# x handed over in both layouts, and LayerNorm's factor applied behind the V, Q and K products

## The chip, the cores and the metric

One NeuronCore of a Trainium2 chip runs the whole program. Its engines are TensorE (PE, with PEld for its weight loads), VectorE (DVE), ScalarE (ACT), GpSimd (POOL) and SyncE (SP), whose queue issues all DMAs here. The metric is the device time of one execution in microseconds (us), lower is better.

## The reference

A transformer block on x of 2048 tokens by 640 features, in float32: pre-LayerNorm sliding-window attention, then a gated MLP. The change touches only the first LayerNorm and the three products behind it.

```python
def _layernorm(x, axis=-1, eps=1e-5):
    m = jnp.mean(x, axis=axis, keepdims=True)
    v = jnp.var(x, axis=axis, keepdims=True)
    return (x - m) / jnp.sqrt(v + eps)

# _A_ref, given x = _layernorm(x): H = 32 heads of Dh = 20, window W = 256
qkv = (x @ wqkv).reshape(B, S, 3, H, Dh).transpose(2, 0, 3, 1, 4)
q, k, v = qkv[0], qkv[1], qkv[2]
scores = einsum("bhqd,bhkd->bhqk", q, k) * Dh ** -0.5   # masked to 0 <= q - k < W
o = einsum("bhqk,bhkd->bhqd", softmax(scores), v)
A = o.transpose(0, 2, 1, 3).reshape(B, S, D) @ wo

h = x + A                                               # A = _A_ref(_layernorm(x))
h2 = h + _B_ref(_layernorm(h))                          # gated MLP, not touched
```

## The kernel before

The order of PE, DVE, ACT and SP is the order of the code (`manual_schedule`); POOL's is set by the framework's scheduler. Each engine works strictly through its list, so an instruction that waits holds all behind it on its engine. That goes for SP too: a DMA that waits for a buffer or for another DMA holds every later one.

Float32 products are made of three matmuls: each operand is split into a high part `hi` (rounded by a copy on ACT) and the rest `lo` (a subtraction on DVE or POOL), and hi*hi, hi*lo and lo*hi are summed in PSUM.

**V stage (0 to 92 us).** The 2048 tokens are 16 tiles of 128. For a tile `load_x` fetches it tokens first; `ln1` takes mean and variance (two `bn_stats`, `bn_aggr`, an addition on DVE, the power -0.5 on POOL) and writes x minus mean times the factor to `xn`; `turn1` transposes `xn` feature first by five PE transposes into two PSUM banks, from which ACT writes `hi` and DVE `lo` (`xn_hi`, `xn_lo`, kept for all tokens); `vgemm` multiplies the tile with Wv, 30 matmuls, and ACT evacuates the two halves. At the start the 640 rows of Wv are split too (`split_wv`, ten pieces). The two halves of the first tile's product wait for these.

**Q and K products (92 to 243 us).** 40 `qk_item`s, for ten blocks `m` of 128 output features and four blocks `c` of 512 tokens: 15 matmuls into one of two PSUM buffers (`pv`). Behind each, `split_qk` splits the result into three bfloat16 parts: ACT (L539), DVE (L541), ACT (L543), POOL (L544), and a store (L547) to the memory tensor `qk_d`. The scores are later taken from `load_stack`'s loads (L299) of `qk_d`. The first 24 items go by block `m`, the last 16 (`dense_tail`) by `c`; among the last, `max_item` makes the first unit's unmasked scores and DVE their row maxima (L339), over a ring of three PSUM banks. Then the main loop of attention starts.

`const`, `tmp` and the like are pools; a `tag` with `bufs=n` is a ring of n buffers, and whoever takes a buffer waits for the last reader of its former content. `tmp` holds the rings `ta` (x tiles, later `sg`), `tb` (`xn`, later `rest`) and `wraw`, `wqh`, `wql` (weights raw, hi, lo).

Of the kernel before, what the change touches and what calls it, by code (L numbers as in the profile page):

```python
# [7 lines left out]
F32 = mybir.dt.float32  # L8
# [25 lines left out]
@with_exitstack  # L34
def block_kernel(ctx, tc, x, wqk, wv, wo, w_in, wsp, bsp, w_out, out):
    nc = tc.nc
# [13 lines left out]
    wo_d = dram.tile([KD, 2, P, D], F32, name="wo_d")  # L50
    r_d = dram.tile([H, S], F32, name="r_d")
    h_d = dram.tile([NT, P, D], F32, name="h_d")
    z1_d = dram.tile([NT, P, FH], F32, name="z1_d")
# [174 lines left out]
    with ExitStack() as ab:  # L228
# [220 lines left out]
        if True:  # L449
# [7 lines left out]

            def ln1(i, between=None):
                xn = tmp.tile([P, D], F32, tag="tb", bufs=2, name=f"xn{i}")
                layernorm(xn, xts.pop(i), D, f"a{i}", between)  # L460
                xns[i] = xn

            def turn1(i):
                xn = xns.pop(i)
                c, o = divmod(i, 4)
                for k0, k1 in ((0, 4), (4, KD)):
                    ps = s2_tile()
                    for k in range(k0, k1):
                        nc.tensor.transpose(ps[:, (k - k0) * P:(k - k0 + 1) * P], xn[:, k * P:(k + 1) * P], ident)
# [3 lines left out]
                    nc.scalar.activation(hi, p3, AF.Copy)  # L473
                    nc.vector.tensor_tensor(out=lo, in0=p3, in1=hi.bitcast(F32), op=OP.subtract)

            def vgemm(i):
                c, o = divmod(i, 4)
                t0 = o * P
                for j in range(2):
                    ps = s1_tile() if j else pv_tile(f"v{i}_{j}")  # L480
                    n0 = j * HD
                    for k in range(KD):
# [5 lines left out]
                    nc.scalar.activation(v4[:, i, 16 * j:16 * j + 16, :DH],  # L488
                                         ps[:, :HD].rearrange("p (h c) -> p h c", c=DH), AF.Copy)

            wqs, raws, after = {}, {}, [iter(())]

            def load_wqk(m):
                raws[m] = tmp.tile([P, KD, P], F32, tag="wraw", bufs=5, name=f"wqraw{m}")
                nc.sync.dma_start(raws[m], wqk[m])
# [9 lines left out]
            def load_wo(k):  # L505
                raws[k] = tmp.tile([P, D], F32, tag="wraw", bufs=5, name=f"woraw{k}")
                nc.sync.dma_start(raws[k], wo[k * P:(k + 1) * P, :])
# [9 lines left out]
            def store_wo(k):  # L517
                for a, t in enumerate(wqs.pop(k)):
                    nc.sync.dma_start(wo_d[k, a], t.bitcast(F32))

            def qk_item(m, c):
                ps = pv_tile(f"qk{m}_{c}")
                hi, lo = wqs[m]
# [12 lines left out]
            def split_qk(m, c, ps):  # L536
                sg = tmp.tile([P, 3, 512], BF16, tag="ta", bufs=3, name=f"sg{m}_{c}")
                rest = tmp.tile([P, 512], F32, tag="tb", bufs=2, name=f"rest{m}_{c}")
                nc.scalar.activation(sg[:, 0, :], ps, AF.Copy)  # L539
                yield  # L540
                nc.vector.tensor_tensor(out=rest, in0=ps, in1=sg[:, 0, :], op=OP.subtract)  # L541
                yield
                nc.scalar.activation(sg[:, 1, :], rest, AF.Copy)  # L543
                nc.gpsimd.tensor_tensor(out=sg[:, 2, :], in0=rest, in1=sg[:, 1, :], op=OP.subtract)  # L544
                T = S // 4
                base = qk_d[m // 5, 0, c // 2, m % 5 * 8, 0, c % 2 * 256:c % 2 * 256 + 256]
                nc.sync.dma_start(bass.AP(tensor=base.tensor, offset=base.offset,  # L547
                                          ap=[[T, P], [2 * 2 * DH * H // 2 * T, 3], [1, 256]]), sg.bitcast(F32))

            halves = [slice(0, HD), slice(HD, D)]  # L550
            load_x(0)
            wv_raw = [tmp.tile([P, D], F32, tag="wraw", bufs=5, name=f"wvraw{k}") for k in range(KD)]
            for j, c in enumerate(halves):
# [12 lines left out]
            for n in range(14):  # L566
                nc.tensor.matmul(warm[:, :P], ident, ident, start=True, stop=True)
            ln1(0)
            split_wv(0, c, nc.vector)
# [5 lines left out]
            for k in (0, 1, 3):  # L575
                split_wv(k, d, nc.gpsimd if k % 2 else nc.vector)
            ln1(1, lambda: [split_wv(k, d, nc.vector) for k in (2, 4)])
            for i in range(NT):
                if i + 3 < NT:
                    load_x(i + 3)  # L580
                if i == 0:
                    vgemm(0)
                    ln1(2, lambda: turn1(1))
                elif i + 2 < NT:
                    ln1(i + 2)
                if i == 1:
# [7 lines left out]
                if 4 <= i <= KD + 3:  # L594
                    store_wo(i - 4)
                if i >= NT - 6 and i < NT - 2:
# [727 lines left out]
```

## Time and profile before

| | us |
|---|---|
| three runs | 1136.86, 1134.21, 1131.7 |
| median | 1134.21 |
| the profiled execution | 1132.73 |
| its span in the profile | 1130.9 |
| PE, DVE, ACT, POOL busy | 1093.7, 732.2, 565.9, 296.6 |

The profile is one execution; its span begins with the first instruction and ends with the last, and 1.8 us of the execution's time lie around it. "Busy" leaves out waiting, register and DMA-issuing instructions. A row of the list in order of time gives start, length, engine, line, operation and tiles, and in brackets the idle time of the engine just before it with what ended it; "x5" are five instructions merged in one row. SPq rows are DMA issues, not transfers. Tile names stand without their numbers.

### The profile page before, as it was taken

What the parts mean: (1) busy time and instruction counts of PE and PEld (TensorE: products, weight loads), DVE (VectorE), ACT (ScalarE), POOL (GpSimd) and SP (SyncE); (2) the same over time, 40 slices, a digit from 0 to 9 for tenths busy, and PEclk for the clock granted to TensorE, in tenths of its full rate; (3) what the DMA queues carried; (4) which work ended last, traced back from release to release, by engine and by line L of the source; (5) the groups of instructions that cost most, each with busy time, mean ns of one, the idle gap of its engine ahead of it and who ended that gap; (6) DMA issues with size and microseconds to landing.
All of it is one profiled execution on the core that took longest, in us unless ns stands there. A gap on an engine that the chain in (4) does not pass through costs nothing.

```text
span 1130.9 us, 28689 instructions
## 1 busy us (share of the span) xinstructions
PE 1093.7 (97%) x11180; PEld 986.3 (87%) x11180; DVE 732.2 (65%) x2060; ACT 565.9 (50%) x1169; POOL 296.6 (26%) x429
## 2 busy tenths in 40 slices
PE   8999999999999999889899999999999899999998
PEld 7998887667887777689799999999999799999998
DVE  6541123789999998478877678645458974656442
ACT  3433443249998989635566567433247521222210
POOL 3314444446666666612200011000001000000000
PEclk9999999999999999999999999999999999999999
DMA  5621346555565555489754522233251564444321
GB/s 183 224 72 68 136 141 239 176 178 170 184 188 175 181 170 158 143 241 305 255 185 165 181 90 76 85 122 101 100 162 57 176 193 135 123 148 138 103 87 61
DMA packets 83320, 171.78 MB, mean 152 GB/s; under 512 B 10944, under 2 KB 45248, under 8 KB 79296
## 3 DMA queue, kind: packets, MB, share of 16 engines
q1 hardware_dynamic: 83184, 169.95, 46.9%
q8 instruction: 88, 1.44, 0.6%
q14 instruction: 48, 0.39, 0.1%
HBM read 112.04 MB, written 57.87 MB: 150 GB/s over the span
## 4 chain that ended last, share of the span: by engine, by line
PE 74%; DVE 7%; DMA 7%; ACT 7%; issue 3%; POOL 1%; SPq 1%; DVEq 0%; ACTq 0%; POOLq 0%
PE g L1064 22%; PE out_ps L1129 8%; PE pv L425 5%; ACT pt L400 4%; PE zb L956 4%; PE qk L525 4%; PE qk L526 4%; PE qk L527 4%; PE bank L329 3%; PE bank L397 3%; PE zx L904 2%; PE zv L904 2%; DMA m<-o_d 2%; DMA wraw<-w_in_in 2%; PE zy L904 1%
## 5 line engine op out<-in xcount | busy, mean ns | idle before, releaser
L400 ACT ACTIVATE pt<-bank 128x384 f32<-128x384 f32 (+1 forms) x452 | 180.7, 477 | 19.9 <-PE bank L397 15.2
L721 ACT ACTIVATE aw<-fx 128x512 fp32r<-128x512 f32 (+2 forms) x160 | 93.5, 594 | 167.3 <-PE g L1064 122.6
L1064 PE MATMUL g<-zl,aw 128*128 128x432 f32 x768 | 171.8, 359 | 0.8 <-ACT zl L721 0.6
L339 DVE CUSTOM_DVE_ANT_0 junk<-bank,strip 128x288 bf16<-128x288 f32 x392 | 156.4, 454 | 14.0 <-PE bank L329 13.0
L1064 PEld LDWEIGHTS g<-zl,aw 128*128 128x128 f32 x768 | 143.7, 188 | 7.6 <-ACT zl L721 0.9
L425 PE MATMUL pv<-pt,v_sb 128*32 128x192 f32 (+3 forms) x1984 | 130.6, 322 | 7.5 <-ACT ot L441 3.5
L1064 PE MATMUL g<-ze,aw 128*128 128x432 f32 x576 | 134.8, 362 | 0.8 <-ACT aw L721 0.4
L715 DVE TENSOR_TENSOR aw<-fx,aw 128x512 fp32r<-128x512 f32 (+2 forms) x160 | 102.6, 646 | 37.9 <-ACT aw L721 36.7
L1064 PEld LDWEIGHTS g<-ze,aw 128*128 128x128 f32 x576 | 107.7, 189 | 7.0 <-ACT aw L721 1.6
L404 POOL TENSOR_SCALAR_AFFINE_SELECT pt<-pt 128x512 f32<-128x512 f32 x128 | 82.3, 644 | 61.9 <-ACT pt L400 58.2
L397 PE MATMUL bank<-slot 123*32 123x288 bf16 (+6 forms) x1296 | 94.0, 275 | 3.1 <-issue 2.2
L1129 PE MATMUL out_ps<-wout,y_sp 128*128 128x320 f32 (+1 forms) x630 | 96.2, 309 | 0.4 <-ACT y_sp L136 0.4
L956 PE MATMUL zb<-win,aw 128*128 128x432 f32 x480 | 95.3, 359 | 0.0
L1129 PEld LDWEIGHTS out_ps<-wout,y_sp 128*128 128x128 f32 (+1 forms) x630 | 94.1, 188 | 1.2 <-ACT y_sp L136 0.7
L329 PE MATMUL bank<-slot 120*32 120x288 bf16 (+6 forms) x1280 | 92.8, 277 | 1.9 <-DVE mcol L339 1.5
L956 PEld LDWEIGHTS zb<-win,aw 128*128 128x128 f32 x480 | 89.9, 187 | 5.0 <-ACT row L721 0.3
L86 POOL TENSOR_TENSOR mvz<-mvz,half 128x1 f32<-128x1 f32 x16 | 10.1, 633 | 303.3 <-DVE mvz L85 303.3
L541 DVE TENSOR_TENSOR rest<-qk,sg 128x512 f32<-128x512 f32 x40 | 27.7, 692 | 84.2 <-ACT sg L539 84.2
L425 PEld LDWEIGHTS pv<-pt,v_sb 128*32 128x32 f32 x1984 | 60.4, 110 | 18.7 <-issue 9.2
L715 DVE TENSOR_TENSOR row<-g,row 128x432 f32<-128x432 f32 x80 | 48.2, 604 | 37.6 <-PE g L1064 36.8
L407 POOL TENSOR_SCALAR_AFFINE_SELECT pt<-pt 128x512 f32<-128x512 f32 x112 | 72.5, 648 | 0.0
L397 PEld LDWEIGHTS <-slot 123*32 123x32 bf16 x1728 | 59.4, 97 | 14.1 <-issue 5.3
(185 smaller groups left out, 2233.0 us busy)
## 6 DMA issues: line engine op xcount, KB each, us to landing
slot<-qk_d SPq DMA_DIRECT2D x144, 160.0 KB
fx<-wsp_in SPq DMA_DIRECT2D x32, 512.0 KB
qk_d<-sg SPq DMA_DIRECT2D x40, 384.0 KB
fx<-hn_d SPq DMA_DIRECT2D x32, 320.0 KB
o_d<-ot SPq DMA_DIRECT2D x64, 128.0 KB
xb<-qk_d SPq DMA_DIRECT2D x48, 160.0 KB
z_d<-row SPq DMA_DIRECT2D x16, 432.0 KB
g_d<-row SPq DMA_DIRECT2D x16, 432.0 KB
```

The source lines that it names most:

```text
L329: nc.tensor.matmul(ps[32 * j:32 * j + 32, o:o + w], one(st, 120, 0, hh, q0, 32), k, start=True, stop=True, tile_position=(0, 32 * j))
L339: nc.vector.tensor_tensor_reduce(out=junk[:, :n], in0=ps[:, :n], in1=keep, scale=1.0, scalar=NEG, op0=OP.add, op1=OP.max, accum_out=m_cols ...
L397: nc.tensor.matmul(ps[32 * i:32 * i + 32, b + o:b + o + w], one(st, 123, 1, hh, k0, 32), q, start=True, stop=True, tile_position=(0, 32 * i))
L400: nc.scalar.activation(pt[:, hh, :n], ps[:, :n], AF.Exp, scale=SCALE)
L404: nc.gpsimd.affine_select(out=pt[:, :, :P], in_=pt[:, :, :P], pattern=[[0, 4], [1, P]], base=0, channel_multiplier=-1, compare_op=OP.is_ge ...
L407: nc.gpsimd.affine_select(out=pt[:, :, 256:], in_=pt[:, :, 256:], pattern=[[0, 4], [-1, P]], base=-1, channel_multiplier=1, compare_op=OP. ...
L425: nc.tensor.matmul(ps[32 * hh:32 * hh + 32, a - 512 * c:b - 512 * c], v_sb[:, kb, v0:v0 + 32], pt[:, hh, a - kb * P:b - kb * P], start=fir ...
L715: (eng or nc.vector).tensor_tensor(out=out, in0=a, in1=b, op=op)
L721: nc.scalar.activation(out, a, AF.Copy)
L956: nc.tensor.matmul(b[0][:, :HF], a[t][:, x, kk], win2[0][:, y, kk, h * HF:(h + 1) * HF], start=kk + x + y == 0, stop=kk == KD - 1 and x == 1)
L1064: nc.tensor.matmul(ps, w[m][:, x, k], zc[k][m][:, y], start=start and k + x + y == 0, stop=stop and k == 3 and x == 1, skip_group_check=True)
L1129: nc.tensor.matmul(ps[j][:, :HD], src[:w, a, k, :], e1["wout"][:w, b, k, j * HD:(j + 1) * HD], start=(k == 0 and a + b == 0), stop=(k == K ...
```

## The change

The host hands over x a second time, as `xt`, tiles of 128 features by 128 tokens. Tiles 0 to 3 go as before (but are only centred, by `center1`, not scaled). Tiles 4 to 15 are loaded both ways: tokens first for the statistics, and feature first for the product. Since the mean lies along the tokens, which now run along the free dimension, it is stored to memory and loaded back to all 128 partitions (`store_mean`, `load_mean`); `turn1` of such a tile subtracts it on DVE, then splits: no PE, no PSUM. The factor `rstd` (`mvs[i][:, 3:4]`) is a scale of ACT's evacuation of V, where tokens are partitions. For Q and K it is stored and loaded to all partitions, 512 tokens at a time (`load_rstd`, one product ahead, into the buffer that becomes `rest`), and a DVE multiply takes the product out of PSUM.

```diff
+            def load_xt(i):
+                t = tmp.tile([P, KD + 1, P], F32, tag="tb", bufs=3, name=f"xt_t{i}")
+                xns[i], rows1[i] = t[:, :KD], t[:, KD]
+                nc.sync.dma_start(xns[i], xt[i])
+
+            def stats1(i):
+                ...
+            def center1(i):
+                xn = tmp.tile([P, D], F32, tag="tb", bufs=3, name=f"xn{i}")
+                nc.vector.tensor_scalar(out=xn, in0=xts.pop(i), scalar1=mvs[i][:, 0:1], scalar2=None,
+                                        op0=OP.subtract)
                 xns[i] = xn
+            def store_mean(i):
+                del xts[i]
+                nc.sync.dma_start(mean_d[i].rearrange("(p a) -> p a", a=1), mvs[i][:, 0:1])
+            def store_rstd(i):
+                nc.sync.dma_start(rstd_d[i].rearrange("(p a) -> p a", a=1), mvs[i][:, 3:4])
+            def every(row, n):
+                return bass.AP(tensor=row.tensor, offset=row.offset, ap=[[0, P], [1, n]])
+            def load_mean(i):
+                nc.sync.dma_start(rows1[i], every(mean_d[i], P))
...
             def turn1(i):
...
+                if i >= TURNED:
+                    hi, lo = (v[c][:, :, o * P:(o + 1) * P] for v in (xn_hi, xn_lo))
+                    nc.vector.tensor_tensor(out=xn, in0=xn, in1=rows1.pop(i)[:, None, :].to_broadcast([P, KD, P]),
+                                            op=OP.subtract)
+                    nc.scalar.activation(hi, xn, AF.Copy)
+                    nc.vector.tensor_tensor(out=lo, in0=xn, in1=hi.bitcast(F32), op=OP.subtract)
+                    return
...
+            def load_rstd():
+                if order:
+                    c = order.pop(0)
+                    rests.append(tmp.tile([P, 512], F32, tag="tb", bufs=3, name=f"rest{len(order)}"))
+                    nc.sync.dma_start(rests[-1], every(rstd_d[4 * c], 512))
             def qk_item(m, c):
+                load_rstd()
...
             def split_qk(m, c, ps):
-                nc.scalar.activation(sg[:, 0, :], ps, AF.Copy)
+                rest = rests.pop(0)
+                nc.vector.tensor_tensor(out=rest, in0=ps, in1=rest, op=OP.mult)
                 yield
-                nc.vector.tensor_tensor(out=rest, in0=ps, in1=sg[:, 0, :], op=OP.subtract)
+                nc.scalar.activation(sg[:, 0, :], rest, AF.Copy)
                 yield
+                nc.vector.tensor_tensor(out=rest, in0=rest, in1=sg[:, 0, :], op=OP.subtract)
                 nc.scalar.activation(sg[:, 1, :], rest, AF.Copy)
...
-            ln1(1, lambda: [split_wv(k, d, nc.vector) for k in (2, 4)])
+            load_x(3)
+            stats1(1)
+            center1(1)
+            load_x(4)
+            for k in (2, 4):
+                split_wv(k, d, nc.vector)
             for i in range(NT):
-                if i + 3 < NT:
-                    load_x(i + 3)
                 if i == 0:
                     vgemm(0)
-                    ln1(2, lambda: turn1(1))
-                elif i + 2 < NT:
-                    ln1(i + 2)
-                if i == 1:
-                    vgemm(1)
-                if 0 < i and i + 1 < NT:
-                    turn1(i + 1)
+                    turn1(1)
+                    for n in (2, 3):
+                        stats1(n)
+                        center1(n)
+                        load_x(n + 3)
+                else:
+                    if i + 3 < NT:
+                        load_xt(i + 3)
+                        load_mean(i + 3)
+                    if i + 6 < NT:
+                        load_x(i + 6)
+                    if i + 1 < NT:
+                        turn1(i + 1)
+                if i + 4 < NT:
+                    stats1(i + 4)
+                    store_mean(i + 4)
+                store_rstd(i)
...
-                if i > 1:
+                if i:
                     vgemm(i)
+            load_rstd()
```

The ring `wraw` shrinks from five buffers to three, two pieces of Wv go to `wqh` for that, and the loads of the Q and K weights are placed accordingly.

**DVE at the start of the V stage.** In the lists of an engine's order a row reads line, operation, output, inputs, size; names carry buffer numbers. Before, from tile 1's statistics on (`mva` are statistics, `slot` is Wv split, `xa` holds hi and lo):

```order
L76 TENSOR_SCALAR mva_197<-mva_197 128x1
L561 TENSOR_TENSOR slot_1_99<-wvraw_129,slot_0_98 128x320
L561 TENSOR_TENSOR slot_1_99<-wvraw_131,slot_0_98 128x320
L80 TENSOR_SCALAR xn_195<-xt_137,mva_197 128x640
L74 BN_STATS sta_244<-xt_144 128x6 x2
L75 BN_AGGR mva_245<-sta_244 128x2
L76 TENSOR_SCALAR mva_245<-mva_245 128x1
L474 TENSOR_TENSOR xa<-bank_118,xa 128x4x128
L474 TENSOR_TENSOR xa<-bank_119,xa 128x128
L80 TENSOR_SCALAR xn_243<-xt_144,mva_245 128x640
```

and after:

```order
L474 TENSOR_SCALAR mva_200<-mva_200 128x1
L479 TENSOR_SCALAR xn_206<-xt_139,mva_200 128x640
L614 TENSOR_TENSOR slot_1_101<-wvraw_131,slot_0_100 128x320
L614 TENSOR_TENSOR slot_1_101<-wvraw_133,slot_0_100 128x320
L514 TENSOR_TENSOR xa<-bank_120,xa 128x4x128
L514 TENSOR_TENSOR xa<-bank_121,xa 128x128
L472 BN_STATS sta_256<-xt_146 128x6 x2
L473 BN_AGGR mva_257<-sta_256 128x2
L474 TENSOR_SCALAR mva_257<-mva_257 128x1
L479 TENSOR_SCALAR xn_263<-xt_146,mva_257 128x640
```

Tile 1's centring moved ahead of the last two weight splits, and tile 2's statistics behind tile 1's remainder `lo`.

**PE at the same place.** Before, behind the last matmul of tile 0's product:

```order
L487 MATMUL bank_117<-slot_0_98,xa 128x320
L469 MATMUL bank_118<-ident,xn_195 128x128 x4
L469 MATMUL bank_119<-ident,xn_195 128x128
L485 MATMUL v_0_272<-slot_0_98,xa 128x320
L486 MATMUL v_0_272<-slot_1_99,xa 128x320
```

and after:

```order
L527 MATMUL bank_119<-slot_0_100,xa 128x320
L509 MATMUL bank_120<-ident,xn_206 128x128 x4
L509 MATMUL bank_121<-ident,xn_206 128x128
L509 MATMUL bank_122<-ident,xn_263 128x128 x4
L509 MATMUL bank_120<-ident,xn_263 128x128
L525 MATMUL v_0_312<-slot_0_100,xa 128x320
L526 MATMUL v_0_312<-slot_1_101,xa 128x320
```

The transposes of tile 2 now stand ahead of tile 1's V product, those of tile 1 where they stood.

**SP where the first stack is loaded**, in the last block `m` ahead of the dense tail. Before:

```order
L299 DMA slot_0_98<-qk_d 20x2048 x4
L495 DMA wqraw_1598<-wqk_in 128x640
L547 DMA qk_d<-sg_0_1589 128x3x256
L299 DMA slot_0_98<-qk_d 20x2048 x4
L547 DMA qk_d<-sg_1_1620 128x3x256
L299 DMA slot_0_98<-qk_d 20x2048 x4
```

and after:

```order
L301 DMA slot_0_100<-qk_d 20x2048 x4
L536 DMA wqraw_1611<-wqk_in 128x640
L569 DMA rest_1613<-rstd_d 128x512
L599 DMA qk_d<-sg_0_1603 128x3x256
L301 DMA slot_0_100<-qk_d 20x2048 x4
L569 DMA rest_1646<-rstd_d 128x512
L599 DMA qk_d<-sg_1_1636 128x3x256
L301 DMA slot_0_100<-qk_d 20x2048 x4
```

One factor load per product stands ahead of the store of the product before.

**DVE at the end of the dense tail.** Before (`junk` rows are row maxima):

```order
L339 ISA junk_15_0_2298,mcol_1_2066<-bank_115,mask 128x384
L339 ISA mcol_1_2066 128x1
L541 TENSOR_TENSOR rest_3_2301<-qk_3_2265,sg_3_2300 128x512
L339 ISA junk_15_1_2305,mcol_1_2066<-bank_117,mask 128x384
L339 ISA mcol_1_2066 128x1
L339 ISA junk_15_2_2311,mcol_1_2066<-bank_116,mask 128x384
```

and after:

```order
L341 ISA junk_15_0_2348,mcol_1_2108<-bank_117,mask 128x384
L341 ISA mcol_1_2108 128x1
L590 TENSOR_TENSOR rest_2271<-qk_3_2314,rest_2271 128x512
L341 ISA junk_15_1_2354,mcol_1_2108<-bank_119,mask 128x384
L341 ISA mcol_1_2108 128x1
L594 TENSOR_TENSOR rest_2271<-rest_2271,sg_3_2350 128x512
L341 ISA junk_15_2_2361,mcol_1_2108<-bank_118,mask 128x384
```

The multiply took the subtraction's place, and the subtraction moved behind the next maximum.

More of the change, by code (lines that the diff above doesn't have):

```diff
@@ L51, in block_kernel @@
     r_d = dram.tile([H, S], F32, name="r_d")
+    mean_d = dram.tile([NT, P], F32, name="mean_d")
+    rstd_d = dram.tile([NT, P], F32, name="rstd_d")
     h_d = dram.tile([NT, P, D], F32, name="h_d")
@@ L551, in block_kernel @@
             load_x(0)
-            wv_raw = [tmp.tile([P, D], F32, tag="wraw", bufs=5, name=f"wvraw{k}") for k in range(KD)]
+            wv_raw = [tmp.tile([P, D], F32, tag=("wraw", "wqh")[k > 2], bufs=(3, 4)[k > 2], name=f"wvraw{k}")
+                      for k in range(KD)]
             for j, c in enumerate(halves):
```

34 lines of the change are left out of this document (23 added, 11 removed).

## The prediction

> **What bounds the kernel now.** I read the page's engine lines first, then busy time by stretch, then the chain that ended last, then the time-ordered list around the stretches that the diff touches.
>
> ```profile
> PE 1093.7 (97%) x11180; PEld 986.3 (87%) x11180; DVE 732.2 (65%) x2060; ACT 565.9 (50%) x1169; POOL 296.6 (26%) x429
> ...
> PE 74%; DVE 7%; DMA 7%; ACT 7%; issue 3%; POOL 1%; SPq 1%; DVEq 0%; ACTq 0%; POOLq 0%
> ```
>
> TensorE (PE) is busy 97% of the span, so a microsecond taken from PE counts where nothing else is late, and one in which PE newly waits counts in full. The stages that the diff touches:
>
> ```profile
> core 0: us, PE busy (x) PEld busy (x) DVE busy (x) ACT busy (x) POOL busy (x), PEclk, DMA share, GB/s
> 24.00:92.00 68.00, 68.00 (x480) 67.94 (x480) 32.24 (x86) 26.21 (x60) 19.01 (x20) 1.00 0.37 126
> ...
> 235.00:240.00 5.00, 5.00 (x25) 3.22 (x24) 4.00 (x15) 1.78 (x3) 1.16 (x1) 1.00 0.60 202
> ```
>
> The row gives each engine's busy time in the stretch with its instructions in brackets, then the granted TensorE clock, the DMA share and GB/s. In the V stage (24 to 92 us) PE never pauses and VectorE (DVE) works 32 us of 68. In the dense tail (the last 16 Q and K products woven with the row maxima, 175 to 243 us) PE is also full, but DVE already works 4.0 of 5 us.
>
> **The transposes.** The chain passes through every tile's five transposes:
>
> ```profile
> 28.25 0.55 PE bank L469 x5
> ...
> 82.68 0.55 PE bank L469 x5
> ...
> 92.72 0.23 PE qk L525
> ```
>
> From the first to the last of these rows are 11 tiles: (82.68 - 28.25) / 11 = 4.95 us a tile, of which 0.55 us is transposing. So a tile without it takes 4.40 us, and 12 tiles give 12 x 0.55 = **6.6 us**, if what replaces the transposes keeps up. In a tile of tile 4 to 15 DVE then runs the statistics and two 128x640 operations on two SBUF tensors, for which the output projection has rows of that shape (the first with the same broadcast operand):
>
> ```profile
> L162 DVE TENSOR_TENSOR m<-m,rs x16: 811/816/1255, 467.9 to 546.7; 128x640 f32<-128x640 f32 x16
> L171 DVE TENSOR_TENSOR xb<-m,xb x16: 814/816/870, 469.9 to 549.1; 128x640 fp32r<-128x640 f32 x16
> ```
>
> Statistics of a tile take 13.46 - 12.23 = 1.23 us (rows below), so DVE needs 1.23 + 2 x 0.82 = 2.9 us of 4.40; even with the slowest row (1.255) twice it is 3.7. ScalarE (ACT) keeps one conversion instead of two and the two evacuations; the factor rides in these as a scale. I cost both at nothing; the cover is PE's 4.40 us, and if it went, the excess would come 12 times.
>
> The means go to memory and come back along partitions. The nearest row of such a trip is the row maxima's:
>
> ```profile
> 247.08 0.41 SPq L354 DMA_DIRECT2D m_d<-m  x1
> 247.59 1.47 SPq L299 DMA_DIRECT2D xb<-qk_d  x2
> 249.55 0.28 SPq L356 DMA_DIRECT2D slot<-m_d  x1
> ```
>
> The store was issued by 247.49, the load that waits for it started at 249.55: 2.1 us to landing. Store, wait, load is about 5 us; the statistics are made three tiles ahead of the centring, 13 us. Queue SP, which waits at the mean's load, carries per tile two loads, a mean load and two 128x1 stores beside the weights: seven or eight issues at about 0.4 us, 3.2 us of 4.40. Hidden, with 1 us to spare in the queue.
>
> **The start of the V stage.** Here the new order costs. The diff puts tile 1's centring before two weight splits on DVE, and the transposes of tile 2 before tile 1's V product on PE.
>
> ```profile
> 12.23 0.87 DVE L74 BATCH_NORM_STATS2 sta<-xt 128x6 f32<-128x320 f32 x2
> ...
> 13.46 0.89 DVE L561 TENSOR_TENSOR slot<-wvraw,slot 128x320 fp32r<-128x320 f32 x2
> ...
> 14.01 0.41 PE L486 MATMUL bank<-slot,xa 128*128 128x320 f32 x1 [0.50 <-DVE slot L561]
> ...
> 14.40 0.61 DVE L80 TENSOR_SCALAR xn<-xt,mva 128x640 f32<-128x640 f32 x1
> ...
> 15.29 0.71 PE L469 MATMUL bank<-ident,xn 128*128 128x128 f32 x5
> ...
> 15.92 0.77 ACT L473 ACTIVATE xa<-bank 128x512 fp32r<-128x512 f32 x2
> ...
> 16.55 0.89 DVE L474 TENSOR_TENSOR xa<-bank,xa 128x512 fp32r<-128x512 f32 x2 [0.31 <-ACT xa L473]
> 16.57 0.41 PE L485 MATMUL v<-slot,xa 128*128 128x320 f32 x1 [0.58 <-ACT xa L473]
> ...
> 33.50 0.39 PE L485 MATMUL v<-slot,xa 128*128 128x320 f32 x1
> ```
>
> PE waits at 14.01 for a weight split on DVE. With the centring (0.61) ahead of it, that and all behind it comes 0.65 us later: transposes of tile 1 at 15.95 to 16.5, and its remainder on DVE, now 1.26 us behind the start of the transposes (16.55 - 15.29, through ACT's conversion), from 17.2 to 18.1. Only then come tile 2's statistics (1.23) and centring (0.61): done at 19.95. PE's next instruction is tile 2's transposes, so it waits from 16.5 to 20.0; tile 1's V product, ready at 18.1, stands behind them. From there: transposes to 20.55, V product 1 to 24.95, tile 3's transposes to 25.5, V products 2 and 3 to 34.3. Tile 4's product then starts at 34.3; in the trace it starts at 33.50. So the start ends 0.8 us later although it has lost two tiles' transposes, and the ten tiles after it gain 10 x 0.55 = 5.5. Net of the V stage: **-4.7 us**.
>
> **The clock.** A PE wait of 3.5 us brings a second price. After the dense tail the trace shows it:
>
> ```profile
> 16.00:20.00 4.00, 3.26 (x20) 3.00 (x21) 2.85 (x10) 1.13 (x3) 1.10 (x2) 1.00 0.76 218
> 242.00:246.00 4.00, 2.39 (x35) 1.00 (x34) 3.65 (x17) 1.43 (x3) 2.96 (x2) 1.00 0.28 98
> 246.00:250.00 4.00, 3.66 (x68) 2.89 (x71) 3.29 (x17) 4.00 (x10) 2.74 (x6) 0.57 0.58 168
> ```
>
> PE was busy 2.39 of 4 us, and in the next 4 us the granted clock was 0.57, that is, 0.5 for 3.4 us; at 3.26 of 4 (16 to 20 us) it stayed at 1.00. A 3.5 us wait leaves PE busy half of some 4 us or less, so I expect a drop. At half clock 3.4 us do the work of 1.7: the price lies between 0 (the drop falls into the wait) and 1.7; I take **+1.2**, nearer the top, since the wait is over soon after a drop can start.
>
> The Trainium skill, page "TensorE: Matmul & The Clock Gate", section "Why this matters for your kernels", advises against PE-idle gaps over about 3 us, because one idle window returns the clock to half. Its Part 1 asks for a free-running window of about 3.4 us of idleness: read strictly, a 3.5 us gap would seldom hold a whole one, and the sum would lack this 1.2. The trace shows the drop behind a stretch that was busy by more than half, so I go by the row.
>
> **Q and K products.** Each of 40 gets a load of 256 KB (the factors, to all partitions) and one more DVE operation, between the product and the split.
>
> ```profile
> 238.16 0.56 DVE L339 CUSTOM_DVE_ANT_0 junk<-bank,mask 128x384 bf16<-128x384 f32 x1 [0.31 <-PE bank L333]
> 238.64 0.08 DVE L339 DVE_READ_ACCUMULATOR2_ANT mcol<- 128x1 f32 x1
> 238.72 0.69 DVE L541 TENSOR_TENSOR rest<-qk,sg 128x512 f32<-128x512 f32 x1
> 239.33 0.55 DVE L339 CUSTOM_DVE_ANT_0 junk<-bank,mask 128x384 bf16<-128x384 f32 x1
> ```
>
> The multiply has the shape and operands of L541: 0.61 us from start to start. In the dense tail L541 comes every 4.40 us (238.72, and 243.12 below), the time of five maxima and one product on PE; DVE waits 0.31 us before most maxima, 1.2 us a product. Multiply, and the subtraction's wait for ACT's 0.60 us conversion behind it (the maximum between them covers 0.5 of it and the hand-over, some 0.3 stay), make 0.9. Hidden, with three score banks of slack. At the tail's end nothing follows to hide it:
>
> ```profile
> 242.42 0.60 ACT L539 ACTIVATE sg<-qk 128x512 bf16<-128x512 f32 x1 [2.34 <-PE qk L527]
> ...
> 243.12 0.69 DVE L541 TENSOR_TENSOR rest<-qk,sg 128x512 f32<-128x512 f32 x1
> 243.73 0.55 DVE L339 CUSTOM_DVE_ANT_0 junk<-bank,mask 128x384 bf16<-128x384 f32 x1
> 244.20 0.55 DVE L339 CUSTOM_DVE_ANT_0 junk<-bank,mask 128x384 bf16<-128x384 f32 x1
> ...
> 244.76 0.24 PE L329 MATMUL bank<-slot 120*32 120x128 bf16 x4 [1.26 <-DVE mcol L339]
> ```
>
> PE waits there for maxima on DVE; multiply and conversion push the last two back by 0.9 us: **+0.9**.
>
> The factor loads. Queue SP is tightest where the first stack is loaded:
>
> ```profile
> 176.21 0.41 SPq L547 DMA_DIRECT2D qk_d<-sg  x1
> 176.67 2.94 SPq L299 DMA_DIRECT2D slot<-qk_d  x4
> ...
> 184.19 1.16 POOL L544 TENSOR_TENSOR sg<-rest,sg 128x512 bf16<-128x512 f32 x1 [2.33 <-ACT sg L543]
> ...
> 236.95 0.37 SPq L547 DMA_DIRECT2D qk_d<-sg  x1
> 237.37 2.21 SPq L299 DMA_DIRECT2D slot<-qk_d  x3
> ```
>
> ```profile
> 180.00:184.00 4.00, 4.00 (x19) 3.23 (x18) 0.69 (x1) 1.73 (x3) 1.76 (x2) 1.00 0.86 323
> ```
>
> Store 0.41, four loads 2.94, and now 0.4 more: 3.8 us for a product of 15 x 0.23 = 3.5 us. Over four products SP falls 1.5 us behind. The load also has the store of the product two back ahead of it in SP, and this waits for GpSimd (POOL), whose subtraction starts some 2.2 us behind its product's end (184.19 for the one that ends at 182.0, ACT, DVE and ACT in between), plus 0.7 for the multiply, and takes 1.16. Followed through, store 0.4, slot loads 2.9, factor load 0.4 and 2.1 to landing bring the worst factors 1 to 2 us after their product's end; the second PSUM buffer allows 3.5 less the multiply. With DMA at 0.86 busy in that stretch a landing may be slower than 2.1 us. Bounds: 0, and 2 us; I take **+0.3**, near hidden, because the slack comes out at about 1 us at the worst product.
>
> **Sum.** -4.7 + 1.2 + 0.9 + 0.3 = -2.3 us. The profiled execution took 1132.73 us (span 1130.9), giving 1130.4; the median of three runs is 1134.21, 1.5 higher, giving 1131.9. I predict **1131**.
>
> **Rivals.**
> 1. The clock stays up at the start. For: the strict reading of the rule; the phase of the window. Against: the row at 246. Sum without 1.2: 1129.2, on the median's scale 1130.7.
> 2. All transposes come out: the start is no later and the clock drop after the dense tail (1.7 us) falls differently and pays for the +0.9 and +0.3. -6.6: 1126.1, on the median's scale 1127.6. Against: the wait at 16.5 follows from a written order.
> 3. Slower: the factor loads are late throughout the dense tail. DVE executes in order, so a multiply that waits for its load holds five maxima behind it, and PE runs out of score banks. Sixteen products late by 0.7 us beyond the slack cost 11, ending at 1141. It decides from about 8 / 16 = 0.5 us a product. For: DMA 0.86 busy and SP full at 176 to 184 us. Against: each load is issued a product (4.4 us) ahead, and in the tail SP is issuing for 0.37 + 2.21 + 0.4 = 3.0 us of that.
>
> **How the numbers follow.** Forecast 0.50, rival 1 0.17, rival 2 0.20, rival 3 0.13. What a measurement of this kernel can tell from no change is about 0.5%, 5.7 us: only rival 2 is faster by that, and a little of rival 1 (0.02); rival 3 is slower; the rest is within. The range goes from rival 2, less 1, to the forecast with both unknowns at their ends (+0.5, +1.7) and half the runs' spread (1131.7 to 1136.86), 2.5, on the median's scale: 1126.5 to 1136.5.
>
> **What would show it.** After: tiles 4 to 14 start 4.40 us apart; one PE gap of 3 to 4 us ahead of tile 2's transposes, released by the centring on DVE, and granted clock near 0.5 within 5 us behind it; the first Q product about 4.7 us earlier, or 3.5 with the drop; the first score of the main loop 0.9 us later against the last Q and K product. PE waiting for a multiply, or the multiply for its load by more than 1 us in many products, would make the prediction wrong; so would DVE or SP running past 4.40 us a tile.

## The result, and the profile after

| | before | after |
|---|---|---|
| median of six runs, us | 1132.95 (1129.69 to 1136.86) | 1206.44 (1201.88 to 1210.05) |
| ratio | | 1.0655, 95% interval 1.0632 to 1.0678 |
| span of the profiled execution, us | 1130.9 | 1206.4 |
| first Q product starts | 91.86 | 162.63 |
| from there to the main loop's first score | 152.90 | 156.97 |
| from there to the end | 886.1 | 886.8 |

The change made the kernel 6.5% slower, where I had forecast 1131. Of the 75.5 us between the two spans the V stage lost 70.8, the Q and K products 4.1. From the page of the kernel after, the engine lines, the granted clock and the DMA share in 40 slices of 30 us, and the chain:

```profile
PE 1114.8 (92%) x11120; PEld 999.4 (83%) x11120; DVE 761.3 (63%) x2088; ACT 568.6 (47%) x1157; POOL 295.5 (24%) x429
...
PEclk9877799999999999999999999999999999999999
DMA  5699667787655556555985452222332455344332
...
PE 62%; DMA 18%; ACT 7%; DVE 7%; issue 3%; SPq 2%; POOL 1%; DVEq 0%; ACTq 0%; POOLq 0%
PE g L1134 21%; DMA mean_d<-mva 9%; PE out_ps L1199 8%; ACT pt L402 5%; PE pv L427 5%; PE zb L1026 4%; PE qk L576 3%; PE qk L577 3%; PE qk L578 3%; PE bank L331 3%; PE bank L399 3%; PE zx L974 2%; PE zv L974 2%; DMA wraw<-w_in_in 1%; DMA o_d<-ot 1%
```

DMA's share of the chain went from 7% to 18%, and half of that is one line, the store of the means. In busy time by stretch, the V stage:

```profile
24.00:92.00 68.00, 43.16 (x224) 39.98 (x223) 17.78 (x42) 14.66 (x27) 11.42 (x12) 0.85 0.84 115
```

PE works 43 us of 68 where it had worked 68, with 224 matmuls for 480. The DMA share went from 0.37 to 0.84 while fewer bytes moved (115 GB/s for 126): the DMA engines are occupied, not carrying. One tile on SP's queue, in order of time, and what DVE and PE wait for there:

```profile
98.02 0.64 SPq L458 DMA_DIRECT2D xt<-x_in  x1
98.76 0.38 SPq L485 DMA_DIRECT2D mean_d<-mva  x1
99.19 0.42 SPq L488 DMA_DIRECT2D rstd_d<-mva  x1
99.71 0.38 SPq L560 DMA_DIRECT2D wo_d<-woh  x1
100.18 0.38 SPq L560 DMA_DIRECT2D wo_d<-wol  x1
100.66 0.41 SPq L465 DMA_DIRECT2D xt_t<-xt_in  x1
108.73 0.32 SPq L494 DMA_DIRECT2D xt_t<-mean_d  x1
```

```profile
101.88 0.83 DVE L501 TENSOR_TENSOR xt_t<-xt_t 128x640 f32<-128x640 f32 x1 [4.91 <-DMA xt_t<-mean_d]
...
103.52 0.63 PE L525 MATMUL v<-slot,xb 128*128 128x320 f32 x1 [4.82 <-ACT xb L503]
```

SP issues the store of the means at 98.76 and everything else of the tile by 101.1; then it stands until 108.73, when that store has landed. Nothing of the next tile is issued before, its loads of x included. A mean load comes about every 11 us (97.65, 108.73), and so does a tile.

### The profile page after: what moved, and what is told of

Its sections match the earlier page's. It is cut to its first block, busy times and chain, and to the rows that moved or that the text cites. A ratio compares the mean times of both kernels' runs of the same rounds, so it can differ in the third digit from the quotient of the medians.

```text
span 1206.4 us, 28772 instructions
## 1 busy us (share of the span) xinstructions
PE 1114.8 (92%) x11120; PEld 999.4 (83%) x11120; DVE 761.3 (63%) x2088; ACT 568.6 (47%) x1157; POOL 295.5 (24%) x429
## 4 chain that ended last, share of the span: by engine, by line
PE 62%; DMA 18%; ACT 7%; DVE 7%; issue 3%; SPq 2%; POOL 1%; DVEq 0%; ACTq 0%; POOLq 0%
PE g L1134 21%; DMA mean_d<-mva 9%; PE out_ps L1199 8%; ACT pt L402 5%; PE pv L427 5%; PE zb L1026 4%; PE qk L576 3%; PE qk L577 3%; PE qk L578 3%; PE bank L331 3%; PE bank L399 3%; PE zx L974 2%; PE zv L974 2%; DMA wraw<-w_in_in 1%; DMA o_d<-ot 1%
## 5 line engine op out<-in xcount | busy, mean ns | idle before, releaser
L427 PE MATMUL pv<-pt,v_sb 128*32 128x192 f32 (+3 forms) x1984 | 133.4, 323 | 8.4 <-ACT ot L443 3.5
L331 PE MATMUL bank<-slot 120*32 120x288 bf16 (+7 forms) x1280 | 92.9, 277 | 3.5 <-issue 1.4
L399 PE MATMUL bank<-slot 123*32 123x288 bf16 (+7 forms) x1296 | 94.8, 275 | 1.1 <-issue 1.1
L427 PEld LDWEIGHTS pv<-pt,v_sb 128*32 128x32 f32 x1984 | 61.5, 110 | 21.8 <-issue 12.2
L596 POOL TENSOR_TENSOR sg<-rest,sg 128x512 bf16<-128x512 f32 x40 | 46.7, 1167 | 87.3 <-ACT sg L595 56.7
```

The lines of the kernel that those rows point to most:

```text
L331: nc.tensor.matmul(ps[32 * j:32 * j + 32, o:o + w], one(st, 120, 0, hh, q0, 32), k, start=True, stop=True, tile_position=(0, 32 * j))
L399: nc.tensor.matmul(ps[32 * i:32 * i + 32, b + o:b + o + w], one(st, 123, 1, hh, k0, 32), q, start=True, stop=True, tile_position=(0, 32 * i))
L427: nc.tensor.matmul(ps[32 * hh:32 * hh + 32, a - 512 * c:b - 512 * c], v_sb[:, kb, v0:v0 + 32], pt[:, hh, a - kb * P:b - kb * P], start=fir ...
```

## Experiments in the V stage: what makes a store of 512 bytes take 10 us

All kernels are edits of the kernel after. My theory was that the 4-byte pieces of the two stores cost this time; the rivals were that any trip through memory does, or the volume of the added loads. The first run gives the means' store pieces of 512 bytes, the second both stores.

```diff
-    mean_d = dram.tile([NT, P], F32, name="mean_d")
+    mean_d = dram.tile([NT, P, P], F32, name="mean_d")
             def store_mean(i):
-                del xts[i]
-                nc.sync.dma_start(mean_d[i].rearrange("(p a) -> p a", a=1), mvs[i][:, 0:1])
+                nc.sync.dma_start(mean_d[i], xts.pop(i)[:, :P])
# in the second also, with rstd_d as [NT, P, P]:
-                nc.sync.dma_start(rstd_d[i].rearrange("(p a) -> p a", a=1), mvs[i][:, 3:4])
+                nc.sync.dma_start(rstd_d[i], ident)
```

> Leaves out the true mean: what is stored for each tile, waited for and loaded back is the first 128 columns of x, as 128 pieces of 512 bytes instead of 128 pieces of 4 bytes; the loads, the waits and their order stay, and so does the factors' store in 4-byte pieces. Theory (a store in 4-byte pieces takes some 8 to 12 us to land, and SP waits for that in every tile): the wait at the mean's load falls to 2 to 3 us, tiles come 4.4 to 6 us apart, and the time is 1130 to 1160 us, the upper end if the factors' 4-byte store, which stays, still occupies the DMA engines. Rival A (any trip through memory costs this much at this place, whatever its pieces): no change, 1200 to 1210. Rival B (the second load of x and the loads to all partitions fill the DMA engines): no change or slower, since more is stored, 1205 to 1215.

> As the run before, and the factors' store too has 128 pieces of 512 bytes (rows of the identity matrix); no 4-byte piece is stored. Leaves out the true mean and factors. Theory: V stage as it was forecast, 4.4 us a tile, the first Q product within 2 us of 87 us, and in all 1130 to 1138, the Q and K stage keeping its 4 us. Rival A (any trip): 1200 to 1210. Rival B (volume of the loads): 1200 or more. A third view, that only the store that is waited for matters, gives the same time here as in the run before, within 2 us.

Then the means' store alone, and both stores with no load that waits for one of them in the code of the V stage:

```diff
# third: no factor store, the factor loads read x
-                nc.sync.dma_start(rstd_d[i].rearrange("(p a) -> p a", a=1), mvs[i][:, 3:4])
+                pass
-                    nc.sync.dma_start(rests[-1], every(rstd_d[4 * c], 512))
+                    nc.sync.dma_start(rests[-1], every(x[c], 512))
# fourth: the mean's load reads x
-                nc.sync.dma_start(rows1[i], every(mean_d[i], P))
+                nc.sync.dma_start(rows1[i], every(x[i], P))
```

> Leaves out the factors' stores; the loads of the factors read a row of x instead. The mean's store stays as it was, 128 pieces of 4 bytes, and is waited for. It tells a price of latency from a price of throughput. If small pieces occupy the DMA engines (some 0.5 us a piece, 8 pieces an engine and store, two stores a tile in 10.8 us), half the load goes and a tile takes 5.4 to 7 us: 1135 to 1155 us. If a store of 4-byte pieces takes its 9 us however little stands beside it, the tile stays near 10 us: 1190 to 1206. Any-trip and load-volume rivals: 1200 to 1206.

> Leaves out the true mean: both stores of 4-byte pieces stay, but the mean's load reads a row of x, so that no load in the V stage waits for a store. Theory with latency alone (the wait in SP is the whole price): 1130 to 1140. Theory with throughput (two stores of 128 small pieces occupy the DMA engines for 8 us a tile, whoever waits for them): the x loads behind them in the same rings come late, tiles take 8 to 10 us, 1170 to 1205. Rival B (volume of the loads): 1200 to 1206.

Measured, one run each beside 1130.42 for the kernel before:

| | us | first Q product at |
|---|---|---|
| after (both stores in 4-byte pieces, mean waited for) | 1206.44 | 162.63 |
| means' store in 512-byte pieces | 1201.93 | 160.35 |
| both in 512-byte pieces | 1139.66 | 92.26 |
| no factor store | 1212.98 | 164.95 |
| no load waits for the mean | 1185.32 | 140.09 |

The second run removes the 70 us, so neither a trip through memory as such nor the volume of the loads makes them (it stores 128 times as many bytes). My theory's number for the first run failed, and the third speaks against a price by throughput: either store alone costs as much as the two together, so the price does not add up over the stores, and it makes no difference whether the store in small pieces is the one that is waited for. The fourth run shows who else is held up. Its code lets no load of the V stage wait for a store, and two thirds of the loss stay (140.09 - 91.86 = 48 us). That doesn't free SP of the stores: in the traces its DMAs signal eight semaphores in turn, and SP issues none before the one that was issued eight places earlier has landed. Of SP's 48 us of waiting between 20 and 90 us, 31 end with the landing of a store; the two largest rows (total, times, longest):

```profile
SPq L548 <- DMA mean_d<-mva: 12.3, 3, 5.7
SPq L485 <- DMA mean_d<-mva: 10.6, 2, 5.9
```

The loads are late themselves: those of x that are issued from 23 us on land 9.8 to 14.7 us after their issue, in the kernel before 2.9 to 4.3. The DMA engines are 97% occupied there, at 133 GB/s:

```profile
24.00:92.00 68.00, 48.01 (x254) 44.78 (x252) 20.74 (x43) 15.49 (x29) 14.48 (x13) 0.82 0.97 133
```

The trace's packet records say who is occupied. The packets of 2560 bytes (x, Wo and their like), from 17 us to the first Q product:

```
                             packets   mean us   median   over 1 us   longest
before                          4015     0.118    0.102           1      1.26
after                           5397     0.274    0.102         360      7.87
means in 512-byte pieces        5404     0.308    0.102         393      8.30
both in 512-byte pieces         5498     0.120    0.102          11      1.35
no factor store                 5504     0.221    0.102         256      7.13
no load waits for the mean      5392     0.318    0.102         462      8.68
```

The 4-byte packets themselves are recorded with 0.01 us in the mean. It is ordinary packets of other transfers that hang, for up to 8.7 us. So one such store holds up other transfers too, which is why it did not matter which store it was or which one the code waits for. How much of the 48 us comes by SP's waits for stores and how much by the late loads alone, no run separates.

What remained was whether a piece is dear because it is small. Three runs tell that: 64-byte pieces side by side; 4-byte pieces 512 bytes apart; and 64 bytes apart.

```diff
# 64-byte pieces side by side (both stores; the factors' is ident[:, :16])
+    mean_d = dram.tile([NT, P, 16], F32, name="mean_d")
+                nc.sync.dma_start(mean_d[i], xts.pop(i)[:, :16])
# 4-byte pieces 512 bytes apart (64 apart: [NT, P, 16]), the factors' store alike
+    mean_d = dram.tile([NT, P, P], F32, name="mean_d")
+                nc.sync.dma_start(mean_d[i][:, 0:1], mvs[i][:, 0:1])
```

> Leaves out the true mean and factors: both stores are 128 pieces of 64 bytes into one stretch of 8 KB (16 columns of x, 16 of the identity matrix); the loads take a row of 512 bytes of it and wait as before. If a piece under 512 bytes always costs the same (a piece's own price): as with 4 bytes, 1195 to 1210. If the price comes from many pieces that fall together into the same small stretch of memory (128 pieces of 4 bytes are one stretch of 512 bytes): between the two, 1140 to 1165. If only 4-byte pieces are dear: 1136 to 1142, as with 512 bytes.

> Leaves out the true mean for the loads and the true factors: both stores still have 128 pieces of 4 bytes, but each lands 512 bytes from the next instead of side by side, so that one store touches 128 stretches of memory and not one; the mean's load reads the first row there (and waits for the store), the factors' loads read a row of x. If the pieces are dear by their size alone: 1195 to 1210. If they are dear because they lie side by side in one stretch and are written one after another: 1136 to 1150, tiles 4.4 to 5 us apart.

> As the run with 4-byte pieces 512 bytes apart, but they land 64 bytes apart, so that eight pieces fall into each stretch of 512 bytes; mean and factor loads read other data as there. Theory (4-byte pieces are dear because neighbours are written into the same small unit of memory one after another): if that unit is 64 bytes, no change against 512 bytes apart, 1133 to 1140; if it is 512 bytes, the eight pieces still follow one another, between 1140 and 1165. If distance had nothing to do with it and the earlier run was quick for another reason: 1195 to 1210.

1135.56, 1136.15 and 1137.91 us, one run each (the kernel before: medians of 1134.43 and 1134.66 beside them). The same 128 pieces of 4 bytes cost nothing that can be seen once they land 64 bytes apart: in these three runs 11 to 17 of some 5500 packets of 2560 bytes take over 1 us, the longest 1.99. My theory of the size falls; what is dear is 128 pieces of 4 bytes side by side in one stretch of 512 bytes. SP's waits, of the kernel after and of the run with 64 bytes between pieces (20 to 90 us; total, times, longest):

```profile
SPq L494 <- DMA mean_d<-mva: 45.2, 6, 9.3
```

```profile
SPq L494 <- DMA mean_d<-mva: 21.5, 12, 3.1
```

7.5 us a tile against 1.8. From the issue of a store to that of the load that it releases it takes 7.6 to 12.2 us side by side (9.8 in the mean of twelve tiles; 108.73 - 98.76 = 10.0 in the rows above), 2.9 to 5.4 us 64 bytes apart (4.0 in the mean). As an estimate, 128 neighbours add some 6 us, 45 ns a piece, as if they were written one after another. That is a reading, not shown: the runs show where the boundary lies (under 64 bytes), not what happens in the memory. Pieces 8 to 32 bytes apart were not tried.

The Trainium skill, page "DMA: Bandwidth & Descriptors", section "Specifications", puts the limit at 512 bytes, under which an engine reads, modifies and writes. By that rule one would expect a price of the stores of 64-byte pieces and of 4-byte pieces far apart too; the runs show none beside 512-byte pieces (1135.56 to 1137.91 us against 1139.66). Its section "Queues, rings and completion order" says that a semaphore's increment lands only after every earlier write of that DMA engine, across queues; that fits the fourth run, where loads of x that have nothing to do with the store are late, though no run shows the mechanism.

## Experiments behind the V stage: the factors

With the stores out of the way the kernel still took 157.5 us from the first Q product to the first score, for 152.9 before. In the run with both stores in 512-byte pieces PE loses 4.0 us in the 17 us in which the first stack is loaded (busy time by stretch; the kernel before, then that run):

```profile
174.86:191.86 17.00, 17.00 (x76) 13.07 (x75) 4.55 (x13) 7.28 (x12) 8.49 (x8) 1.00 0.72 263
```

```profile
175.26:192.26 17.00, 12.98 (x53) 9.63 (x53) 6.73 (x9) 6.08 (x10) 6.54 (x5) 1.00 0.84 288
```

and DVE's multiply waits for its factors there (172 to 195 us of the same run):

```profile
DVE rest L589 <- DMA rest<-rstd_d: 9.4, 3, 4.3
...
PE qk L575 <- DVE rest L589: 4.0, 4, 1.2
```

Four kernels from that run: no factors on Q and K (these products and their split as in the kernel before); the factor load ahead of the four stack loads; loads of a quarter of the bytes; and one factor tile kept in SBUF.

```diff
# load first: load_rstd() moved from the start of qk_item to its end
                 after[0] = split_qk(m, c, ps)
                 next(after[0])
+                load_rstd()
# a quarter (multiply reads the row four times)
-                    nc.sync.dma_start(rests[-1], every(rstd_d[4 * c], 512))
+                    nc.sync.dma_start(rests[-1][:, 512:], every(rstd_d[4 * c], P))
# resident: loaded once, used by all 40 multiplies
+                    if not rests:
+                        rests.append(tmp.tile([P, P], F32, tag="fac", bufs=1, name="fac"))
+                        nc.sync.dma_start(rests[-1], every(rstd_d[4 * c], P))
```

The first of the texts that follow gives 159.7 us for this stage in the run with both stores in 512-byte pieces; its trace has 157.55.

> The run with both stores in 512-byte pieces, without the factor on Q and K: no factor loads, no multiply, Q and K split straight from PSUM as in the kernel before. It tells what the factors cost behind the V stage. If the factors cost the whole loss there (in that run the first stack's loads of the main loop hold the factor loads up, PE loses 4.0 us between 175 and 190 us, and the tail some 2 more): PE full between 172 and 192, the time from the first Q product to the first score of the main loop back from 159.7 to 153 us, 1131 to 1134 in all. If the V stage's second reading of x is what is late there: no more than 2 us gained, 1137 to 1139.

> The run with both stores in 512-byte pieces, with each factor load one place earlier on SP: ahead of the four stack loads that follow a product instead of behind them. Same loads, same bytes. If the order on SP makes the factors late (four stack loads of 3.5 us ahead of each): DVE's multiply no longer waits for them, PE loses under 1 us between 172 and 192 us instead of 4.0, 1134 to 1137. If the DMA engines' load there makes them late (DMA share 0.78 to 0.88, 277 to 295 GB/s): the waits stay, 3 to 4 us, 1138 to 1141.

> The run with both stores in 512-byte pieces, with factor loads of 64 KB instead of 256 KB: the same number of loads at the same places, each fetches the factors of 128 tokens to all partitions, and the multiply uses these four times. If the bytes make the factors late where the first stack is loaded (store 384 KB, stack 640 KB and factors 256 KB are 1.28 MB a product, at the 290 GB/s seen there 4.4 us, while PE takes 3.5): 1.09 MB and 3.7 us a product remain, PE loses 0.5 to 1.5 us there instead of 4.0, and the Q and K stage takes 153.5 to 155 us instead of 157.5. If a load's latency or SP's order makes them late: as before, 157 us.

> The run with both stores in 512-byte pieces, without the 40 factor loads: one load of 64 KB ahead of the Q and K stage stays in SBUF, and every multiply uses the factors of those 128 tokens. The multiply, its place on DVE and the chain behind it stay. If all of the stack's 4.0 us comes from the factor loads, by bytes or by order: PE full between 172 and 192 us, and the Q and K stage takes 153.3 to 154 us, its rest over 152.9 being the multiply at the tail's end. If the longer chain through the multiply itself (it holds PSUM for another hand-over in DVE) makes products late: 155 to 157 us.

| | stage, us | PE busy in the 17 us | ratio to before, 95% interval |
|---|---|---|---|
| before | 152.90 | 17.00 | |
| both stores in 512-byte pieces | 157.55 | 12.98 | one run |
| no factors | 152.76 | 17.00 | 0.9997 (0.9975 to 1.0019) |
| load first | 157.13 | 14.50, clock 0.90 | 1.0036 (1.0007 to 1.0065) |
| a quarter of the bytes | 155.52 | 14.86 | 1.0026 (0.9998 to 1.0054) |
| resident | 152.71 | 17.00 | 0.9985 (0.9960 to 1.0010) |

The run with the resident tile settles the cause: the multiply, its place on DVE and the longer chain cost nothing, and the 40 loads of 256 KB cost it all. How they do is settled less well. A quarter of the bytes halves the loss of 4.0 us to 2.1, more than the 0.5 to 1.5 that I expected to be left. An earlier place on SP shows no gain: DVE waits 11.9 us for factors at the stack (9.4 before the move), PE gets through 55 matmuls in the 17 us for 53, and the stage is no shorter. PE's longer busy time there is a drop of the clock (0.90 over 17 us is 1.7 us of work). So the bytes have a part, and the order that was tried has none that can be seen; what makes the rest was not separated.

One candidate is SP's round of eight semaphores. With the factors a product has six DMAs there instead of five, and in the run with both stores in 512-byte pieces the factor loads issued from 170 to 187 us land 5.2 to 6.1 us after their issue. Six such landings with eight in flight take, as an estimate, 6 x 5.7 / 8 = 4.3 us, for a product of 3.5; five at the 5.3 to 6.0 us of the stack loads in the kernel before come out at 3.5. No run tests this.

## A version without the trips

The last version keeps x in both layouts and lets PE put mean and factor along the free dimension. Tiles 0 to 3, the start of the stage, V's evacuation, Q and K are as in the kernel before; nothing of the statistics goes to memory.

```diff
                 if i >= TURNED:
                     hi, lo = (v[c][:, :, o * P:(o + 1) * P] for v in (xn_hi, xn_lo))
+                    ps = s2_tile()
+                    for a, (j, op) in enumerate(((0, OP.subtract), (3, OP.mult))):
+                        nc.tensor.transpose(ps[:, a * P:(a + 1) * P], mvs[i][:, j:j + 1].to_broadcast([P, P]), ident)
+                    for a, op in enumerate((OP.subtract, OP.mult)):
+                        row = ps[:, a * P:(a + 1) * P]
+                        nc.vector.tensor_tensor(out=xn, in0=xn, in1=row[:, None, :].to_broadcast([P, KD, P]), op=op)
```

> A version that keeps x in both layouts and drops every trip through memory: for tiles 4 to 15 two PE transposes of a column (mean, factor), spread over 128 columns, put both along the free dimension on all partitions of one PSUM bank, and DVE subtracts the one row and multiplies by the other before the split. Tiles 0 to 3, the start of the stage, and Q, K and V's evacuation are as in the kernel before. A tile trades five transposes (0.55 us) for two (0.22), 12 x 0.33 = 4.0 us; DVE has 1.23 + 3 x 0.82 = 3.7 us of work in a tile of 4.6 us. Theory: first Q product near 88 us, 1126 to 1128 against 1130 to 1132 in the kernel before, ratio 0.996 to 0.997. Rival (the second reading of x, 320 KB a tile, or DVE at 3.7 us makes tiles late): as before or slower, 0.999 to 1.003.

1129.8 us against 1134.66 beside it (medians), ratio 0.9961 (0.9938 to 0.9984): faster than both kernels by what the tiles promise. Its first and last rows of the pair of transposes in 60 to 87 us, its V stage, and its first Q product:

```profile
63.85 0.38 PE L488 MATMUL bank<-ident,mva 128*128 128x128 f32 x2
...
77.70 0.38 PE L488 MATMUL bank<-ident,mva 128*128 128x128 f32 x2
```

```profile
24.00:86.00 62.00, 62.00 (x431) 61.85 (x431) 42.86 (x82) 24.38 (x47) 18.82 (x20) 1.00 0.61 203
```

```profile
86.72 0.39 PE L554 MATMUL qk<-xa,wqh 128*128 128x512 f32 x1
```

Three tiles in 13.85 us are 4.62 a tile for 4.95, so 12 x 0.33 = 4.0 us; PE never pauses, and DVE's 43 of 62 us and the second reading of x stay hidden. The first Q product is 5.1 us earlier; the 1.1 beyond the tiles lies in the start of this one execution, where tile 1's V product begins at 15.40 instead of 16.57.

## Why the prediction was wrong, step by step

**The round trip of the means: the step that failed.** The prediction took "2.1 us to landing" from the row maxima's store (24 KB), called a trip of 5 us under 13 us of lead "Hidden, with 1 us to spare in the queue", and put nothing into the sum or the range for it. In the kernel after, the load is issued 7.6 to 12.2 us behind the store, and SP waits for most of that (7.5 us a tile), so the lead of three tiles was worth nothing: the loads that should run ahead stand behind the wait. The store that I measured the trip by is of another form, and the form is the price. Even with 4-byte pieces 64 bytes apart it is 2.9 to 5.4 us where I had 2.1 and an issue, and SP's spare microsecond is used up by 1.8 us of waiting a tile. In the run with both stores in 512-byte pieces DVE waits 12.8 us for mean loads, PE loses 2.3 us of 68 (a wait and a stretch of that run below), and the V products of tiles 10 to 13 start 4.95 to 6.10 us behind the one before, 3.8 us more in all than at 4.40. So without the dear store the first Q product comes at 89.4 to 92.3 us in eight runs, where I had forecast 87.2 to 88.4. That share of the step was a size; the 70 us were the form of the store. The last sentence of the prediction named the sign to look for (SP running past 4.40 us a tile), but no rival gave it a price.

```profile
DVE xt_t L500 <- DMA xt_t<-mean_d: 12.8, 8, 2.8
```

```profile
24.00:92.00 68.00, 65.70 (x439) 64.22 (x439) 32.87 (x69) 28.39 (x51) 20.81 (x19) 1.00 0.78 247
```

**The transposes, -6.6.** Right in size: in the run with both stores in 512-byte pieces the V products of tiles 3 to 9 start 4.40 us apart with PE full. Behind tile 9 the waits just named take 3.8 of the 6.6 back.

**The start, +0.8 net of two tiles' transposes.** Right to 0.1 us. Forecast were a wait of PE until 20.0 and the start of tile 3's V product at 29.9 (34.3 less one tile):

```profile
19.98 0.77 PE L509 MATMUL bank<-ident,xn 128*128 128x128 f32 x5 [3.19 <-DVE xn L479]
...
29.93 0.31 PE L525 MATMUL v<-slot,xa 128*128 128x320 f32 x1
```

**The clock, +1.2.** Neither right nor wrong: it is 0 or, by half of a 3.4 us window, 1.7. The granted clock changes on a grid of 3.413 us. The windows of the grid around the same PE wait (PE busy is the second number, the granted clock the third from the end), first the kernel after, then the run with 64-byte pieces:

```profile
18.19:21.60 3.41, 1.62 (x12) 1.62 (x13) 3.27 (x12) 0.77 (x2) 1.16 (x2) 1.00 0.17 34
21.60:25.02 3.42, 3.42 (x26) 3.41 (x25) 3.12 (x11) 0.53 (x1) 1.05 (x3) 1.00 0.50 163
```

```profile
17.81:21.22 3.41, 1.42 (x11) 1.42 (x12) 3.27 (x12) 0.72 (x2) 0.95 (x2) 1.00 0.14 22
21.23:24.64 3.41, 3.41 (x15) 3.41 (x14) 3.27 (x11) 0.56 (x2) 1.16 (x2) 0.50 0.65 184
```

The same wait of 3.2 us falls 0.4 us differently into the grid, and in the one execution the next window runs at half clock, in the other not. In four of the twelve profiled executions with this wait (that of the kernel after among them) the clock stayed, in eight it fell. Rival 1 had the profiled execution right, by its "phase of the window".

**The Q and K products, +0.9 and +0.3.** The 0.9 at the tail's end was 0: from the last Q or K matmul to the first score it is 319.60 - 316.88 = 2.72 us, for 2.82 before, since that score now waits for POOL and not for the maxima:

```profile
319.60 0.24 PE L331 MATMUL bank<-slot 120*32 120x128 bf16 x4 [1.17 <-POOL xb L296]
```

The 0.3 for the factor loads at the first stack was 4.1: the right place and the right wait, mis-sized because I counted SP's issues (0.4 us) and a landing of 2.1, and not what four stack loads, a store and 256 KB of factors ask of the DMA engines in a product's 3.5 us. The factor loads issued there, from 240 to 254 us of the kernel after, land 5.5 to 6.4 us after their issue. The trace of the kernel before would have told: its stack loads issued from 172 to 179 us take 5.3 to 6.0. The bound of 2 us that I gave was too low. Rival 3 had the mechanism, but in the dense tail, where no such wait came.

**The range.** Its upper end rested on the clock and on the factor loads; an operation with no row of its kind (a store in 4-byte pieces) was taken at the row of another kind, without a bound on the dear side.

## What to carry to other kernels

A column of one value per partition, stored side by side to memory, is a dear DMA however few bytes it has: it holds up other transfers too, so the lead did not hide it, and taking the wait for it out of the code left two thirds of the loss. Put such a column along the free dimension by PE (two transposes of 0.11 us here), or keep the pieces 64 bytes apart. And price a wait on an in-order queue by all that stands behind it: a lead of three tiles is gone when the loads that make it are issued behind the wait.

## What the runs showed of the hardware

A 512-byte store of 128 neighbouring 4-byte pieces took 7.5 to 12.2 us to land in the kernel after, and up to 16.9 where no load waits for it. Beside such stores 2560-byte packets of other transfers, 0.1 us in the median, took as much as 8.7. With the same pieces 64 bytes apart the stores landed within 5.4 us, and no such packet took over 2.0.

The granted clock went with PE's busy time in one window of a fixed grid of 3.413 us. Over the windows that hold the end of the start's wait, it fell in the eight executions with PE busy for 0.29 to 1.42 us of 3.41, and stayed in the four with 1.53 to 1.93. The Trainium skill, page "TensorE: Matmul & The Clock Gate", Part 1, describes a free-running window of that length, which agrees, and has the clock fall after an idle window; here it fell after windows that were 42% busy. The busy time is not the whole rule: in the kernel after, the clock fell behind a window with 1.80 us (154.71 to 158.13), and in the kernel before behind the dense tail with 1.68 (242.71 to 246.13), part of it the scores' matmuls on 32 columns. Whether narrow matmuls count for less was not tried.
